# Feed-forward accumulators in four one-bank PSUM tiles, and a new order at the ends of the turns

## Chip, cores and metric

One NeuronCore of one Trainium2 chip runs the whole program. The metric is device time in microseconds (us) of one execution, median of several runs. PE is the matrix engine (TensorE), DVE the vector engine, ACT the scalar engine, POOL GpSimd, and SP the engine whose queue issues most DMAs.

## What is computed

Attention with rotary positions, then a feed-forward block with a squared ReLU, then a gated one, all in fp32 (each fp32 product is made of three passes over a high and a low part):

```python
q_rot, k_rot = rotate(q), rotate(k)                    # q, k, v: (4, 8, 576, 64)
attn = softmax(q_rot @ k_rot.T / 8)
x = (attn @ v).transpose(0, 2, 1, 3).reshape(2304, 512)

r = maximum(x @ w_in, 0)                               # w_in:  (512, 2048), w_out: (2048, 512)
x = (s * r * r + b) @ w_out

g = x @ w_gate                                         # w_gate, w_val: (512, 1536)
return (silu(g) * (x @ w_val)) @ w_out2                # w_out2: (1536, 512)
```

## The kernel before

A planner in the kernel (`Schedule`) holds a list of operations, each with an engine, an assumed duration, a priority, its dependencies, and tokens for the buffers that it takes (`acq`) and gives back (`rel`). `run` walks through modelled time and, on each engine, emits the operation of lowest priority number that is ready and finds its buffers free. What it emits is the order of the instructions on each engine; each engine then works strictly in that order, and the builder adds the semaphore waits that the data and the buffers ask for, tile by tile. So a change of a priority, a dependency or a pool moves instructions all over the later program.

After the attention part the work comes in these stages:

- Block B (`block_b`, which calls `moe1`): the first 512 tokens through the first feed-forward block, in 16 chunks of 128 hidden units. For each chunk, twelve matmuls make `h` (`hb<-x,w`, L844 to L846), ACT and DVE make the activation as a high part `gh` (L901) and a low part `gl` (L906), and twelve matmuls add it into four accumulators (`acc<-gh,w`, the same lines).
- Turn blocks (`block_s(1)`, `block_s(2)`): 768 and 1024 tokens, in two halves. Products of prepared tokens and weights (`hb<-w`) serve both halves in a scheme with seven products in place of eight; `combine` makes the weight pieces (additions L1134, high parts L1140, low parts L1142), `x_load_s` loads the attention result (L1044) and its normalizers (L1059) and prepares the tokens (additions and products L1071, low parts L1083). The first half is accumulated along with the products; its four accumulators are copied out (`y<-acc`, L1194 on DVE and L1196 on ACT); then the second half is accumulated from stored activations, 16 chunks of twelve matmuls (`gh` L1212, `gl` L1215). I call these two parts the first and the second turn.
- Gated blocks (`block_2`, three of them): the same with the second feed-forward block, 768 tokens each, two turns, second projection at L1453 to L1455, copies `o<-acc` at L1468 (DVE) and L1470 (ACT), output DMAs at L1476, token preparation at L1368 to L1379.

PSUM has eight banks. Four are single-bank tiles: three of pool `t` and one of pool `v`, used for `hb`. The other four are two tiles of two banks each, pool `ps_s`: the attention scores use them, and all accumulators after that, two in a tile:

```python
t = ps_s.tile([128, 1024], F32, tag="s", name="acc")
st["acc", h, d], st["acc", h, d + 1] = t[:, 0:QS], t[:, 512:512 + QS]
```

In the gated blocks, which have three accumulators, the second turn starts in the fourth bank, `(c + 3) % 4`. `behind` is what a following block's token preparation waits for in the plan: an activation near the end of the first turn.

Of the kernel before, what the change touches and what calls it, by code (L numbers as in the profile page):

```python
# [8 lines left out]
F32 = mybir.dt.float32  # L9
# [168 lines left out]
def tile_attention_moe_moe(  # L178
# [61 lines left out]
    ps_s = ctx.enter_context(tc.tile_pool(name="ps_s", bufs=2, space=PSUM))  # L240
# [7 lines left out]
    att = ExitStack()  # L248
    at_c = att.enter_context(tc.tile_pool(name="at_c", bufs=1))
# [598 lines left out]
    chains = {"ga": ([], []), "gb": ([], [])}  # L848

    def moe1(st, n, chunks, outs, x_toks, xp, prio, h_pools, get_h, rounds, acc_tok, get_acc, per_bank, gp, rp, pool, engs, rate=1):  # L850

        step = 0
        pend = None
        held = []
        hs, order = chains[gp]
        fin = {}

        def second(pend, rd, first, last):
            f, gops, g_tok, gi = pend
            for z, d in enumerate(rounds[rd]):  # L860
                def fn(z=z, d=d):
                    if first and z == 0:
                        st.setdefault("acc", {}).update(zip(rounds[rd], get_acc(len(rounds[rd]))))
# [3 lines left out]
                    mm3(st["acc"][d], w[:, 0, cs], w[:, 1, cs], gh, gl, first and z % per_bank == 0, last and (z + 1) % per_bank == 0)  # L867
                fin[d] = op("pe", t_mm(n, 3), fn, prio + step * rate, (*gops, W_op["out", f], *order[-1:]), acc_tok[rd] if first and z == 0 else (),
                            (g_tok, W_tok["out", f]))
                order.append(fin[d])  # L870

        for ci, f in enumerate(chunks):
# [11 lines left out]
            r_tok, g_tok = Token(rp), Token(gp)  # L884
            sq_eng = engs
            ew = min(prio + step * rate, EWA) if gp == "ga" else prio + step * rate
            def relu(ci=ci):
                st["g", ci] = tuple(pool(gp).tile([128, 512], F32R, tag=tag, name=tag)[:, 0:n] for tag in ("gh", "gl"))
                st["r", ci] = pool(rp).tile([128, 512], F32, tag="r", name="r")[:, 0:n]
# [33 lines left out]
        for rd in range(1, len(rounds)):  # L923
            for pend in held:
                step += len(rounds[rd])
                second(pend, rd, pend is held[0], pend is held[-1])
# [11 lines left out]
    def switch():  # L938
# [4 lines left out]
        pool("gc", 1)  # L943

# [17 lines left out]
    def block_b():  # L962
# [8 lines left out]
        toks = (Token("s"), Token("s"))  # L971

        def get_acc(m):
            res = []
            for _ in range(2):
                t = ps_s.tile([128, 1024], F32, tag="s", name="acc")
                res += [t[:, 0:UB], t[:, 512:512 + UB]]
            return res

        fin = moe1(st, UB, range(F1), outs, x_toks, xp, prio, ("t", "v"), get_hb,  # L980
                   (tuple(range(KD)),), (toks,), get_acc, 1, "gb", "rb2", lambda name: late[name], "act")
        y_op[0] = []
        for d in range(KD):
            y_tok = Token("rb2", "rc")
            def ev(d=d, y_tok=y_tok):
                st["y", d] = late[y_tok.pool].tile([128, 512], F32, tag="r", name="y")[:, 0:UB]
                nc.scalar.activation(out=st["y", d], in_=st["acc"][d], func=AF.Copy)
            o = op("act", t_act(UB), ev, prio + 900, (fin[d],), (y_tok,), (toks[d // 2],))
# [158 lines left out]
    def block_s(i):  # L1147
# [251 lines left out]
    def block_2(i):  # L1399
# [185 lines left out]

        if not EARLY:
            close()
# [86 lines left out]
```

## Time and profile before

| | us |
|---|---|
| median of 3 runs | 1109.14 |
| lowest and highest run | 1108.8, 1109.45 |
| the profiled execution | 1112.42 |
| its span, first to last instruction | 1110.6 |
| PE busy in the span | 1085.3 (98%), 6218 matmuls |
| DVE busy | 898.2 (81%) |
| ACT busy | 738.6 (67%) |
| mean granted clock of TensorE | 0.995 |

"Busy" is the union of the instructions' times. Matmuls overlap in the pipeline and their ends are modelled, so two matmuls that follow each other without a gap are started one every 0.17 to 0.23 us while each is shown 0.34 to 0.40 us long. What a stretch costs is therefore read from the starts of the matmuls. An idle time in a row is counted from the end of the instruction before on the same engine, with what ended it behind `<-`.

### The profile page before, as it was taken

Reading aid. Unit: us, or ns where it says so; the run is one execution under the profiler, and the core shown is the slowest. Engines: PE = TensorE matmul, PEld = TensorE weight load, DVE = VectorE, ACT = ScalarE, POOL = GpSimd, SP = SyncE. Lnnn points to the kernel's source line nnn. Section 1 sums busy time; section 2 is a strip of 40 time slices with the busy share of each in tenths; the row PEclk is TensorE's granted clock in tenths of the full one; section 3 lists DMA queues with packets and bytes.
Section 4 is the critical chain, followed back from the end, with each engine's and each line's share of the span. In section 5 each row is a group of like instructions: output and inputs, shape, how many; then the busy total and the mean of one; then the engine's idle time right before and its main releaser. Section 6 shows DMA issues by size and latency. Waiting matters only on the chain.

```text
span 1110.6 us, 17632 instructions
## 1 busy us (share of the span) xinstructions
PE 1085.3 (98%) x6218; PEld 986.3 (89%) x6218; DVE 898.2 (81%) x1575; ACT 738.6 (67%) x1511; POOL 202.9 (18%) x166
## 2 busy tenths in 40 slices
PE   8999999999999999989999999999999999999998
PEld 7899999999888799989888878999889998899986
DVE  6999999999988998779899887786586675866750
ACT  5998998999877875546565646665555554655550
POOL 7898877522310000000000000000000000000000
PEclk9999999999999999989999999999999999999999
DMA  4556865654569544572456644231331122311101
GB/s 122 198 187 236 276 213 196 204 183 152 174 206 270 166 163 161 161 199 86 159 189 207 213 160 143 86 114 57 89 92 38 58 81 66 99 41 51 45 17 41
DMA packets 110681, 155.51 MB, mean 140 GB/s; under 512 B 33905, under 2 KB 66689, under 8 KB 110593
## 3 DMA queue, kind: packets, MB, share of 16 engines
q1 hardware_dynamic: 109776, 153.60, 43.3%
q8 instruction: 49, 0.80, 0.3%
q10 hardware_dynamic: 816, 0.79, 0.2%
q14 instruction: 40, 0.32, 0.1%
HBM read 99.98 MB, written 32.58 MB: 119 GB/s over the span
## 4 chain that ended last, share of the span: by engine, by line
PE 85%; DVE 8%; ACT 3%; DMA 2%; issue 1%; SPq 1%; POOL 0%; ACTq 0%; DVEq 0%; POOLq 0%
PE hb L844 13%; PE hb L846 13%; PE hb L845 13%; PE acc L844 6%; PE acc L845 6%; PE acc L846 6%; PE ps_s L652 6%; PE acc L1453 4%; PE acc L1455 4%; PE acc L1454 4%; PE ps_t L713 4%; PE ps_av L743 3%; PE ps_av L745 2%; DVE nm L655 2%; DVE pl L728 2%
## 5 line engine op out<-in xcount | busy, mean ns | idle before, releaser
L844 PE MATMUL hb<-w 128*128 128x384 f32 (+1 forms) x728 | 251.2, 345 | 1.1 <-ACT tmp L1512 0.9
L846 PE MATMUL hb<-w 128*128 128x384 f32 (+1 forms) x728 | 250.4, 344 | 0.0
L845 PE MATMUL hb<-w 128*128 128x384 f32 (+1 forms) x728 | 250.1, 344 | 0.0
L844 PEld LDWEIGHTS hb<-w 128*128 128x128 f32 x728 | 136.7, 188 | 11.5 <-ACT tmp L1512 3.3
L845 PEld LDWEIGHTS hb<-w 128*128 128x128 f32 x728 | 136.7, 188 | 7.4
L846 PEld LDWEIGHTS hb<-w 128*128 128x128 f32 x728 | 136.7, 188 | 4.5
L844 PE MATMUL acc<-gh,w 128*128 128x512 f32 (+1 forms) x320 | 120.8, 377 | 4.9 <-DVE y L1194 3.4
L845 PE MATMUL acc<-gl,w 128*128 128x512 f32 (+1 forms) x320 | 120.1, 375 | 0.7 <-DVE gl L906 0.7
L846 PE MATMUL acc<-gh,w 128*128 128x512 f32 (+1 forms) x320 | 120.1, 375 | 0.0
L655 DVE TENSOR_REDUCE nm<-ps_s 128x1 f32<-128x576 f32 x144 | 108.2, 752 | 8.0 <-PE ps_s L652 6.4
L659 ACT ACTIVATE e<-ps_s,nm 128x576 f32<-128x576 f32 x144 | 106.8, 742 | 8.7 <-DVE nm L655 7.0
L721 ACT ACTIVATE ph<-ps_t 128x512 fp32r<-128x512 f32 x192 | 105.6, 568 | 9.3 <-PE ps_t L713 7.4
L652 PE MATMUL ps_s<-t,a 128*128 128x288 f32 x320 | 99.3, 327 | 4.6 <-ACT e L659 4.4
L743 PE MATMUL ps_av<-ph,vh 128*128 128x384 f32 (+1 forms) x320 | 98.3, 329 | 0.9 <-DVE ph L728 0.5
L728 DVE TENSOR_TENSOR pl<-ps_t,ph 128x512 fp32r<-128x512 f32 x144 | 95.5, 683 | 1.0 <-ACT ph L721 0.2
L1512 ACT ACTIVATE tmp<-hb 128x384 f32<-128x384 f32 x144 | 70.3, 488 | 35.1 <-PE hb L846 33.5
L652 PE MATMUL ps_s<-kz,a 128*128 128x288 f32 x320 | 89.0, 294 | 0.0
L713 PE MATMUL ps_t<-ident,e 128*128 128x128 f32 x576 | 85.7, 273 | 1.9 <-DVE a L565 1.2
L745 PE MATMUL ps_av<-pl,vh 128*128 128x384 f32 (+1 forms) x256 | 75.6, 306 | 0.0
L1142 DVE TENSOR_TENSOR w<-sums,w 128x512 fp32r<-128x512 f32 x104 | 68.5, 686 | 8.1 <-ACT w L1140 8.0
L844 PEld LDWEIGHTS acc<-gh,w 128*128 128x128 f32 x320 | 61.2, 191 | 14.9 <-DVE y L1194 5.1
L713 PEld LDWEIGHTS ps_t<-ident,e 128*128 128x128 f32 x576 | 67.7, 140 | 6.7 <-issue 1.4
(128 smaller groups left out, 2404.9 us busy)
## 6 DMA issues: line engine op xcount, KB each, us to landing
raw<-gv SPq DMA_DIRECT2D x36, 512.0 KB, 3.6
raw<-in_moe_w_out_dram SPq DMA_DIRECT2D x28, 512.0 KB, 3.7
x_d<-xr SPq DMA_DIRECT2D x32, 288.0 KB, 2.7
raw<-in_moe_w_in_dram SPq DMA_DIRECT2D x16, 512.0 KB, 4.4
raw<-up SPq DMA_DIRECT2D x16, 512.0 KB, 4.3
raw<-in_moe_w_gate_dram SPq DMA_DIRECT2D x12, 512.0 KB, 4.2
raw<-in_moe_w_val_dram SPq DMA_DIRECT2D x12, 512.0 KB, 4.2
gv<-dec SPq DMA_DIRECT2D x24, 256.0 KB, 2.2
```

The source lines that it names most:

```text
L652: nc.tensor.matmul(ps[:, hf * 512:hf * 512 + HS], a[:, q0:q0 + 128], m[:, k0:k0 + HS], start=y == 0, stop=y == len(todo) - 1)
L655: nc.vector.tensor_reduce(out=st["nm"][:, u:u + 1], in_=st["s", u], axis=AX.XY, op=ALU.max, negate=True)
L659: nc.scalar.activation(out=st["e", u].rearrange("p (f n) -> p f n", f=2), in_=st["s", u], func=AF.Exp, bias=st["nm"][:, u:u + 1], accum_ou ...
L713: nc.tensor.transpose(ps[:, z * 128:z * 128 + 128], st["e", u][:, kc * 128:kc * 128 + 128], ident)
L721: nc.scalar.activation(out=st["ph", y][0:rows, 512 * i:512 * i + n], in_=st["pt", y, i][0:rows, 0:n], func=AF.Copy)
L728: nc.vector.tensor_tensor(out=dst, in0=st["pt", y, i][0:rows, 0:n], in1=st["ph", y][0:rows, c].bitcast(F32), op=ALU.subtract)
L743: nc.tensor.matmul(ps, vv, st["ph", y][:, c], start=kc == 0, stop=kc == 4)
L745: nc.tensor.matmul(ps, vv, st["pl", y][:, c], start=False, stop=False)
L844: nc.tensor.matmul(o, lh, rh, start=first, stop=False, skip_group_check=more)
L845: nc.tensor.matmul(o, lh, rl, start=False, stop=False, skip_group_check=more)
L846: nc.tensor.matmul(o, ll, rh, start=False, stop=last, skip_group_check=more)
L1512: nc.scalar.activation(out=st[key, f], in_=ps[name], func=AF.Copy)
```

## The change

1. The pool `ps_s` is closed with the attention part, and a pool `acc` of four tiles of one bank each is opened in its place. Each accumulator takes a tile and gives it back by itself.
2. In block B, an activation may use the buffers `gb` or `gc` and `rb2` or `rc`; and in the second to last chunk no second projection is placed, so that those of the last three chunks follow the last `h`.
3. In the turn blocks the first accumulator of the second turn takes a bank of `t` or `v` (an `hb` bank). The first unit's weight combination gets a priority ahead of the token preparation.
4. `behind` also holds the copies of the first turn: the following block's token preparation is placed behind them.
5. In the gated blocks, the activations of the first two chunks of the second turn are formed before the last one of the first turn, in the last block too, and the second turn's first accumulator gets those two before the first turn is closed. The very last copy is done in two halves of 256 columns, one on ACT and one on DVE.

```diff
-    ps_s = ctx.enter_context(tc.tile_pool(name="ps_s", bufs=2, space=PSUM))
+    ps_s = att.enter_context(tc.tile_pool(name="ps_s", bufs=2, space=PSUM))
...
+        pool("acc", 4, space=PSUM)
+
+    def get_acc(n):
+        return late["acc"].tile([128, 512], F32, tag="acc", name="acc")[:, 0:n]
...
-            if pend is not None:
-                second(pend, 0, pend[3] == 0, False)
-                step += len(rounds[0])
-            pend = (f, (o1, o2), g_tok, ci)
-            held.append(pend)
-        second(pend, 0, len(chunks) == 1, True)
+            pend.append((f, (o1, o2), g_tok, ci))
+            while len(pend) > 1 and ci != len(chunks) - 2:
+                x = pend.pop(0)
+                second(x, x[3] == 0, False)
+                step += KD
+        second(pend[0], False, True)
...
-                ("up", u), prio + 60 * (u - 2) + 30, (kept["in", 2 * u], kept["in", 2 * u + 1], W_op["in", F1 - 1], W_op["out", F1 - 1]), (prev,),
+                ("up", u), prio - (701 if i == 1 else 341) if u == 0 else prio + 60 * (u - 2) + 30, (kept["in", 2 * u], kept["in", 2 * u + 1], W_op["in", F1 - 1], W_op["out", F1 - 1]), (prev,),
...
-        acc_tok = {(h, e): Token("s") for h in range(2) for e in range(2)}
+        acc_tok = {(h, d): Token("t", "v") if (h, d) == (1, 0) else Token("acc") for h in range(2) for d in range(KD)}
...
-                    if f == 0 and d % 2 == 0:
-                        t = ps_s.tile([128, 1024], F32, tag="s", name="acc")
-                        st["acc", h, d], st["acc", h, d + 1] = t[:, 0:QS], t[:, 512:512 + QS]
+                    if f == 0:
+                        st["acc", h, d] = get_hb(acc_tok[h, d], QS) if (h, d) == (1, 0) else get_acc(QS)
...
-        behind[i + 1] = pend[1][0]
-        finish(0, fin, prio + 60 * U + 10)
+        behind[i + 1] = (*pend[1][0], *finish(0, fin, prio + 60 * U + 10))
...
-                    o = st["bank"][c if h == 0 else (c + 3) % 4]
+                    o = st["acc", h, c]
...
+                wide = 256 if last and c == nt - 1 else 512
+                both = []
+                for m in range(0, 512, wide):
+                    on_dve = c % 2 or m > 0
...
-        EARLY = 0 if last else 2
-        behind[NB + i + 1] = pend[0]
+        EARLY = 2
...
+            behind[NB + i + 1] = *pend[0], *finish(0, out_proj(0, F2 - 1, prio + 60 * F2 + 10, *pend), prio + 60 * F2 + 10, False)
...
-            o1 = op("act", t_act(QN, False), high, pr, (u2s[f], last_high if f >= max(EARLY, 1) else prev_high), (g_tok,))
+            o1 = op("act", t_act(QN, False), high, pr, (u2s[f], last_high if f >= EARLY else prev_high), (g_tok,))
```

How the order moves, at three places. First DVE at the end of block B, from the next to last low-part of the token preparation on (`gl` is block B's last one, `w<-w` is token preparation, `sums` and the `w` behind them are weight pieces of the turn block). Before:

```order
L1083 TENSOR_TENSOR w<-w 128x768
L906 TENSOR_TENSOR gl<-r,gh 128x512
L1134 TENSOR_TENSOR sums<-raw 128x256
L1083 TENSOR_TENSOR w<-w 128x768
L1142 TENSOR_TENSOR w<-raw,w 128x512
L1134 TENSOR_TENSOR sums<-sums,raw 128x256
L1142 TENSOR_TENSOR w<-raw,w 128x256
L1134 TENSOR_TENSOR sums<-raw 128x256 x2
L1134 TENSOR_TENSOR sums<-raw,sums 128x256
L1142 TENSOR_TENSOR w<-raw,w 128x512
L1134 TENSOR_TENSOR sums<-sums,raw 128x256
L1142 TENSOR_TENSOR w<-sums,w 128x512 x2
```

The same place in the change, where these lines are L1074, L905, L1125 and L1133, and L1062 is an addition of the token preparation:

```order
L905 TENSOR_TENSOR gl<-r,gh 128x512
L1125 TENSOR_TENSOR sums<-raw 128x256
L1133 TENSOR_TENSOR w<-raw,w 128x512
L1125 TENSOR_TENSOR sums<-sums,raw 128x256
L1062 TENSOR_TENSOR w<-w 128x768
L1125 TENSOR_TENSOR sums<-raw 128x256
L1074 TENSOR_TENSOR w<-w 128x768
L1125 TENSOR_TENSOR sums<-raw,sums 128x256
L1074 TENSOR_TENSOR w<-w 128x768
L1133 TENSOR_TENSOR w<-raw,w 128x256
L1133 TENSOR_TENSOR w<-sums,w 128x512 x2
```

One L1071 and one L1083 moved from before the last `gl` to behind it, and one L1142 and two L1134 of the second unit's weights moved behind `w<-sums`.

Second, DVE between the turns of the first turn block: the last `gl`s of the first turn's end, the two copies, and the token preparation of the next block. Before:

```order
L1071 TENSOR_TENSOR w<-w 128x1024
L1215 SCALAR_TENSOR_TENSOR gl<-w,bv,gh 128x384
L1194 COPY y<-acc 128x384
L1071 TENSOR_TENSOR w<-w 128x1024
L1194 COPY y<-acc 128x384
L1215 SCALAR_TENSOR_TENSOR gl<-w,bv,gh 128x384
L1071 TENSOR_TENSOR w<-w 128x1024 x2
```

In the change (L1207 is `gl`, L1184 the copy, L1062 the preparation):

```order
L1207 SCALAR_TENSOR_TENSOR gl<-w,bv,gh 128x384 x2
L1184 COPY y<-acc 128x384 x2
L1062 TENSOR_TENSOR w<-w 128x1024
L1207 SCALAR_TENSOR_TENSOR gl<-w,bv,gh 128x384
L1062 TENSOR_TENSOR w<-w 128x1024
L1207 SCALAR_TENSOR_TENSOR gl<-w,bv,gh 128x384
L1062 TENSOR_TENSOR w<-w 128x1024
L1207 SCALAR_TENSOR_TENSOR gl<-w,bv,gh 128x384
L1062 TENSOR_TENSOR w<-w 128x1024 x2
```

The preparation moved from among the copies to behind them. Before, each copy on DVE waits for ACT; in the change for PE alone.

Third, DVE's last instructions in the change, with the semaphores that they wait for (L1587 forms the last block's stored low parts):

```order
L1587 TENSOR_TENSOR w<-w 128x384 [waits Activation_49] x3
L1455 COPY o<-acc 128x512 [waits DVE_49,PE_49]
L1587 TENSOR_TENSOR w<-w 128x384 [waits Activation_49] x4
L1587 TENSOR_TENSOR w<-w 128x384 [waits DVE_49,Activation_49]
L1455 COPY o<-acc 128x512 [waits DMAHW6_49,DMAHW7_49,DVE_49,PE_49]
L1455 COPY o<-acc 128x256 [waits DMAHW1_49,DMAHW0_49,Activation_49]
```

The last one is DVE's half of the last accumulator, and waits for ACT; before, ACT copied all of it and DVE had no such instruction.

## Rows read from the trace of the kernel before

**Rows 1.** Waits of PE from 330 us on: in total, times, longest.

```profile
PE acc L844 <- DVE y L1194: 3.4, 2, 2.9
PE acc L1453 <- DVE o L1468: 2.4, 3, 0.8
PE acc L844 <- ACT gh L901: 1.3, 1, 1.3
PE hb L844 <- ACT tmp L1512: 0.9, 4, 0.4
...
PE acc L1453 <- ACT o L1470: 0.7, 1, 0.7
```

**Rows 2.** Timeline of PE, end of block B: start, duration, instruction, idle before.

```profile
379.76 0.39 PE L845 MATMUL acc<-gl,w 128*128 128x512 f32 x1
379.99 0.39 PE L846 MATMUL acc<-gh,w 128*128 128x512 f32 x1
381.70 0.50 PE L844 MATMUL acc<-gh,w 128*128 128x512 f32 x1 [1.32 <-ACT gh L901]
...
387.15 0.34 PE L844 MATMUL hb<-w 128*128 128x384 f32 x1
...
389.24 0.33 PE L844 MATMUL hb<-w 128*128 128x384 f32 x1
```

**Rows 3.** Busy time in a window: PE, PEld, DVE, ACT, POOL, granted clock, DMA.

```profile
380.00:390.00 10.00, 7.95 (x31) 6.38 (x30) 10.00 (x21) 8.67 (x17) 0.00 (x0) 0.83 0.26 95
```

**Rows 4.** Timeline of PE between the turns of the first turn block.

```profile
479.02 0.34 PE L846 MATMUL acc<-gh,w 128*128 128x384 f32 x1
...
489.29 0.33 PE L846 MATMUL acc<-gh,w 128*128 128x384 f32 x1
```

**Rows 5.** Timeline of DVE at the same place.

```profile
482.00 1.23 DVE L1071 TENSOR_TENSOR w<-w 128x1024 f32<-128x1024 f32 x1 [2.57 <-DMA w<-x_d]
483.15 0.55 DVE L1194 COPY y<-acc 128x384 f32<-128x384 f32 x1
...
488.32 2.36 DVE L1071 TENSOR_TENSOR w<-w 128x1024 f32<-128x1024 f32 x2 [0.97 <-DMA w<-x_d]
```

**Rows 6.** Timeline of PE between the turns of the first gated block.

```profile
800.22 0.39 PE L1455 MATMUL acc<-w,gl 128*128 128x512 f32 x1
800.68 0.50 PE L1453 MATMUL acc<-w,gh 128*128 128x512 f32 x1
...
801.25 0.40 PE L1455 MATMUL acc<-w,gl 128*128 128x512 f32 x1
802.43 0.50 PE L1453 MATMUL acc<-w,gh 128*128 128x512 f32 x1 [0.78 <-DVE o L1468]
```

**Rows 7.** Timeline of DVE at the same place.

```profile
801.68 0.69 DVE L1468 COPY o<-acc 128x512 f32<-128x512 f32 x1 [0.79 <-PE acc L1455]
```

**Rows 8.** Timeline of DVE, end of block B.

```profile
381.32 0.95 DVE L1083 TENSOR_TENSOR w<-w 128x768 fp32r<-128x768 f32 x1
382.19 0.68 DVE L906 TENSOR_TENSOR gl<-r,gh 128x512 fp32r<-128x512 f32 x1
...
386.28 0.69 DVE L1142 TENSOR_TENSOR w<-raw,w 128x512 fp32r<-128x512 f32 x1
386.88 0.42 DVE L1134 TENSOR_TENSOR sums<-sums,raw 128x256 f32<-128x256 f32 x1
387.21 1.29 DVE L1142 TENSOR_TENSOR w<-sums,w 128x512 fp32r<-128x512 f32 x2
```

**Rows 9.** Groups of DVE, 479 to 519 us: busy us, mean ns, idle before.

```profile
L1071 DVE TENSOR_TENSOR w<-w 128x1024 f32<-128x1024 f32 x10 | 12.0, 1220 | 3.5 <-DMA w<-x_d 3.5
L1215 DVE SCALAR_TENSOR_TENSOR gl<-w,bv,gh 128x384 fp32r<-128x384 f32 x14 | 8.6, 615 | 1.1 <-ACT gh L1212 1.0
L1083 DVE TENSOR_TENSOR w<-w 128x1024 fp32r<-128x1024 f32 x7 | 8.4, 1220 | 0.0
```

**Rows 10.** Groups of ACT, 470 to 520 us, and ACT's last copy in the timeline.

```profile
L1196 ACT ACTIVATE y<-acc 128x384 f32<-128x384 f32 x4 | 2.0, 488 | 3.7 <-DMA raw<-up 2.8 <-PE acc L846 0.9
...
1106.49 0.60 ACT L1470 ACTIVATE o<-acc 128x512 f32<-128x512 f32 x1 [17.07 <-PE acc L1455]
```

More of the change, by code (lines that the diff above doesn't have):

```diff
@@ L846, in mm3, with moe1, second, fn @@
         nc.tensor.matmul(o, ll, rh, start=False, stop=last, skip_group_check=more)
-    chains = {"ga": ([], []), "gb": ([], [])}
-    def moe1(st, n, chunks, outs, x_toks, xp, prio, h_pools, get_h, rounds, acc_tok, get_acc, per_bank, gp, rp, pool, engs, rate=1):
+    chains = {"gb": ([], [])}
+    def moe1(st, n, chunks, outs, x_toks, xp, prio, h_pools, get_h, acc_tok, gp, rp, pool, engs, rate=1):
         step = 0
-        pend = None
-        held = []
-        hs, order = chains[gp]
+        pend = []
+        hs, order = chains["gb"]
         fin = {}
-        def second(pend, rd, first, last):
+        def second(pend, first, last):
             f, gops, g_tok, gi = pend
[L860 to L863, printed above, removed]
+            for d in range(KD):
+                def fn(d=d):
+                    if first:
+                        st["acc", d] = get_acc(n)
                     w = W["out", f]
@@ L866, in fn @@
                     gh, gl = st["g", gi]
-                    mm3(st["acc"][d], w[:, 0, cs], w[:, 1, cs], gh, gl, first and z % per_bank == 0, last and (z + 1) % per_bank == 0)
-                fin[d] = op("pe", t_mm(n, 3), fn, prio + step * rate, (*gops, W_op["out", f], *order[-1:]), acc_tok[rd] if first and z == 0 else (),
+                    mm3(st["acc", d], w[:, 0, cs], w[:, 1, cs], gh, gl, first, last)
+                fin[d] = op("pe", t_mm(n, 3), fn, prio + step * rate, (*gops, W_op["out", f], *order[-1:]), (acc_tok[d],) if first else (),
                             (g_tok, W_tok["out", f]))
@@ L883, in moe1, with relu @@
                 step += 1
-            r_tok, g_tok = Token(rp), Token(gp)
+            r_tok, g_tok = Token(*rp), Token(*gp)
             sq_eng = engs
[L886 to L889, printed above, removed]
+            ew = prio + step * rate
+            def relu(ci=ci, r_tok=r_tok, g_tok=g_tok):
+                st["g", ci] = tuple(pool(g_tok.pool).tile([128, 512], F32R, tag=tag, name=tag)[:, 0:n] for tag in ("gh", "gl"))
+                st["r", ci] = pool(r_tok.pool).tile([128, 512], F32, tag="r", name="r")[:, 0:n]
                 nc.scalar.activation(out=st["r", ci], in_=st["h", ci], func=AF.Relu)
@@ L1180, in fn @@
                     mm3(st["acc", h, d], w[:, 0, cs], w[:, 1, cs], gh, gl, f == 0, f == F1 - 1)
-                res.append(op("pe", t_mm(QS, 3), fn, pr + d, (*gops, W_op["out", f], *order[-1:]), (acc_tok[h, d // 2],) if f == 0 and d % 2 == 0 else (),
+                res.append(op("pe", t_mm(QS, 3), fn, pr + d, (*gops, W_op["out", f], *order[-1:]), (acc_tok[h, d],) if f == 0 else (),
                               (g_tok, W_tok["out", f])))
@@ L1429, in bank @@
             return p.tile([128, 512], F32, tag=tag, name="hb")[:, 0:QN]
-        a_toks = (Token("s"), Token("s"))
-        evs = {}
-        def get():
-            st["bank"] = []
-            for _ in range(2):
-                t = ps_s.tile([128, 1024], F32, tag="s", name="acc2")
-                st["bank"] += [t[:, 0:512], t[:, 512:1024]]
+        a_toks = {(h, c): Token("acc") for h in range(2) for c in range(nt)}
         def out_proj(h, f, pr, gops, g_tok, chunks=None):
-            def need(c):
-                return (evs[0, c - 1],) if h == 1 and f == 0 and c > 0 else ()
             res = []
@@ L1446, in fn @@
                 def fn(c=c):
-                    if f == 0 and c == 0 and h == 0:
-                        get()
+                    if f == 0:
+                        st["acc", h, c] = get_acc(512)
                     w = o_st[f]
@@ L1476, in put @@
                         e.dma_start(out=out[b * S:(b + 1) * S].rearrange("(r g) m -> r g m", g=PC)[:, g], in_=st["y", h, c][64 * z:64 * z + 64])
-                    sch.dma(131072, put, pr, (o,), (), (y_tok,), eng="act" if other else "sp")
+                    sch.dma(131072, put, pr, both, (), (y_tok,), eng="act" if other else "sp")
+            return evs
         t_tok = {}
```

63 lines of the change are left out of this document (27 added, 36 removed).

## The prediction

> **What bounds the kernel now.** I read the page first: TensorE (PE) has work in flight for 1085.3 of 1110.6 us, so a gain can only come out of stretches in which PE starts nothing. PE's list of waits after the attention part gives those that this change touches, all around the accumulators of the feed-forward blocks [rows 1]: the copies `y` on DVE, the copies `o` on DVE and on ACT, and an activation `gh` of the first block. These rows count idle time from the modelled end of a matmul; what a wait costs is read from the starts. Undisturbed, PE starts a 512-column matmul every 0.23 us and a 384-column one every 0.174 us (387.15 to 389.24 are twelve steps) [rows 2].
>
> Place A, the end of block B. From 379.99 to 387.15 PE starts 13 matmuls in 7.16 us [rows 2]; 13 x 0.227 = 2.95, so 4.21 us are lost, part of it as a lower clock: the granted clock is 0.83 in that 10 us stretch, some of it at the lower of its two levels after the idle time, while DVE has work for 10.00 of 10.00 us [rows 3]. PE waits there for the last chunk's activations.
>
> Place B, between the two turns of the first turn block (`block_s(1)`). From 479.02 to 489.29 PE starts 24 matmuls in 10.27 us [rows 4]; 24 x 0.174 = 4.18, so 6.09 us are lost. DVE's timeline tells why: an addition of the token preparation (L1071) sat 2.57 us for a load from `x_d`, and the copy L1194 that PE needs stood behind it and came at 483.15 [rows 5]; PE's longest wait for it is 2.9 us [rows 1].
>
> The other places: the second wait for `y` is 3.4 - 2.9 = 0.5 [rows 1]. At 800.68 the step is 0.46 in place of 0.23 (0.23 lost), and at 802.43 it is 1.18 (0.95 lost, of which 0.78 is shown as idle, so a shown wait costs about 0.17 more than it says) [rows 6]. The `o` L1468 wait occurs three times (2.4 in all) and the `o` L1470 one once (0.7) [rows 1]. DVE's copy at 801.68 had itself been held 0.79 us by PE [rows 7]: it reads one bank of a two-bank tile, and waited for matmuls into the other bank.
>
> **The change part by part, by place.**
>
> *A, activations a step ahead.* Twelve more matmuls (the second projection of the chunk before) stand between the last first-projection matmul and the last second projection; no matmul is added. So the last activations have 24 x 0.227 = 5.45 us where they had 2.7. But DVE is full. Before the last `gl`, the order takes two preparation instructions away, 0.87 us each (381.32 to 382.19), so `gl` ends at about 382.87 - 1.74 = 381.1 where PE would reach it at 380.45: 0.7 us of waiting stay. The next thing that is late is the weight piece `sums` (L1142) for the third product of the turn block; in before it starts at 387.21. The change takes one L1142 and two L1134 from in front of it, 0.60 + 0.33 + 0.33 = 1.27 us [rows 8]; the first unit's combination is also planned ahead of the token preparation, but DVE still must do all of both. So it ends at 387.21 - 1.27 + 0.69 = 386.6, and the third product starts at about 386.7, not 389.24 [rows 2]. Gain 2.55 of 4.21, 1.65 stay. Bounds: nothing gained if DVE had to do the same work in front of it, all 4.21 if it found room. I take the middle because the two lists of DVE are known instruction by instruction and DVE has no idle time there.
>
> *B, preparation behind the copies.* Two additions (L1071, 1.22 us each [rows 9]) that stood among the last `gl`s of the first turn move behind the two copies; the two copies follow each other. Nobody in front of a copy waits for a load any more. The first accumulator of the second turn gets a bank of its own kind (an `hb` bank), the other three follow copies that are 3, 6 and 9 matmuls old, so the entry costs nothing. What waits next: the addition that needs the last `x_d` piece now holds `gl`s of the second turn. In before the addition could start at 488.32, after 0.97 us of waiting for the load, which is 9.1 us after the turn's first matmul (nominally 479.02 + 0.17 = 479.2) [rows 4, 5]. The SP queue of the change issues the loads of the first token rows later and the following ones earlier, with the same bytes; I take 6.7 to 9.1 us. Behind it stand one multiplication and `gl` of chunk 5: 2 x 1.15 + 0.6 later, 9.6 to 12.0, and PE wants it after five chunks of 12 x 0.174, at 10.4. Then two multiplications and the next `gl`, 2.9 against PE's 2.1: 0.8 more. So 0 to 2.4 us of waiting, I take 1.2. Gain 6.09 - 1.2 = 4.9; if the loads come 1 us later than in before, 3.5 stay.
>
> *One bank for each accumulator, and the turn order of the gated blocks.* The second `y` wait goes with its 0.17: 0.67. In each of the two inner gated turns (800 and the same at 942) both steps go, 2 x 1.18 = 2.36: the first copy no longer waits for the neighbouring bank's matmuls, and the second starts when its own bank is done, about a step and a half before PE wants it. In the last block the wait of 0.7 (0.87) goes because two chunks of the second turn are now done before the close, and the third L1468 wait (0.95) because a free bank is taken. Together 4.85. What covers the copies, if they were later: nine matmuls, 2 us.
>
> *Fewer waits for buffers in block B* (`gc` and `rc` added to the choices): no wait of PE names them; 0, from -0.5 to 0.5.
>
> *The last copy in two halves.* The last ACT copy takes 0.60 us, and the last DMA is issued straight behind it [rows 10]. The halves are 256 columns. From the 384-column copies, 0.49 on ACT [rows 10] and 0.55 on DVE [rows 5], and the 512-column ones, 0.60 and 0.69 [rows 7, 10], 256 columns are 0.38 and 0.42 (estimates along the slope). The built order makes DVE's half wait for ACT's: 0.80 + 0.04 = 0.84, so 0.24 us are lost. Side by side they would end after 0.42 and win 0.18. The Trainium skill (PSUM — Partial Sum Buffer, section on bank collisions) says that two engines must not touch one bank in the same partitions at the same time, two reads included, while different banks are free: by that, halves of one bank have to take turns, and only halves of two banks would win. The wait in the order agrees; without it the sum below would be 0.4 us lower.
>
> Everything else is moved, not added: PE has the same number of matmuls, DVE one instruction more. The waits of products for `tmp` (0.9 in all [rows 1]) I leave as they are.
>
> Sum: 2.55 + 4.9 + 4.85 - 0.24 = 12.1 us. The profiled execution's span is 1110.6 and it took 1112.42 us; the median of the runs is 1109.14, 3.3 below it. Taken off the span, 1098.5; off the median, **1097.0 us**.
>
> **The rivals.** *All of it comes back*: DVE finds room at A and the loads land early at B. 4.21 + 6.09 + 4.85 + 0.2 = 15.35 off: 1093.8. For it: neither wait is one for arithmetic that PE depends on by nature. Against it: DVE's 10.00 of 10.00.
>
> *DVE becomes the bound at the entries of the turn blocks*: the third product at A comes no earlier than now (4.21 stay), B keeps 3.5, and the reshuffled DVE order costs another 1 us somewhere later. 15.15 - 8.7 - 0.24 = 6.2 off: 1102.9. For it: in the second turn at B, DVE has 12 L1071 and 7 L1083 of 1.22, 16 `gl` of 0.615 [rows 9] and about 4.2 of weights, 37 us, in a turn of 192 x 0.174 = 33.4. Against it: the last 5 us of this are needed only after the third product of the next block, 2.7 us past the turn's end.
>
> *Slower, by that same queue*: with the preparation wholly inside the second turn, a late load delays every `gl` behind it, then the next block's products, and the clock falls again. By the count above it has some 1 us of slack beyond a landing at 9.1 us; each further us is a us of PE. It turns the whole change slower by over 2.2 us when that piece lands 14 us later, about 23 us into the turn: then about 1112. For it: the loads in front of it are all in one queue, and their order is changed. Against it: nothing adds bytes.
>
> *Nothing happens*: the builder still ties the copies to neighbours or the planner's new order makes as many small waits as it takes away: 1109. Against it: the DVE copies of the change wait for PE alone.
>
> **How the numbers follow.** Forecast 0.60; all back 0.12; DVE the bound 0.17; nothing 0.05; slower 0.06. A measurement of this kernel tells about 0.2%, 2.2 us, from no change (its runs lie within 0.7 us). Faster: 0.60 + 0.12 + 0.17 = 0.89; the same 0.05; slower 0.06. The range takes in the full return (1093.8, less 0.3) and the DVE case (1102.9, plus 0.6): 1093.5 to 1103.5, and leaves out the last two cases and the tails.
>
> **What would show it.** PE's waits without `y` and `o`; at B the copies on DVE side by side with nothing between them, and a wait of PE for `gl` (L1207 in the change) of 0 to 2.4 us some 10 us into the turn; at A a `gl` wait of 0.7 and a wait of a product for a weight piece of about 1; a granted clock of 1.0 around both; DVE's 256-column copy starting as ACT's ends. Wrong would be: PE waits of over 4 us for `gl` or for products at the next block's entry, or the copies still starting after other engines' work.

## The result and the profile after

The change takes the median from 1109.3 us (4 runs, 1108.8 to 1113.51) to **1098.03 us** (4 runs, 1096.49 to 1099.74). The ratio is 0.9891 with a 95% interval of 0.9862 to 0.9919: faster by 0.8 to 1.4%. The forecast was 1097.0, in a range of 1093.5 to 1103.5. The total came out near the forecast; its parts did not, as the runs below show.

The head of the profile page and the busy times of the changed kernel:

```profile
span 1096.5 us, 17621 instructions
## 1 busy us (share of the span) xinstructions
PE 1078.2 (98%) x6218; PEld 984.6 (90%) x6218; DVE 897.3 (82%) x1576; ACT 736.7 (67%) x1511; POOL 204.8 (19%) x166
```

PE's waits from 330 us on, against [rows 1]:

```profile
PE hb L844 <- ACT tmp L1237: 0.5, 1, 0.5
PE hb L844 <- ACT w L1237: 0.4, 1, 0.4
```

All waits for `y`, `o`, `gh`, `gl` and for the gated blocks' `tmp` are gone in this profile, the last also, which the forecast had left standing. Two short ones are new: products at the entry of the first turn block, in PE's timeline (against [rows 2]):

```profile
388.34 0.34 PE L846 MATMUL hb<-w 128*128 128x384 f32 x1
389.16 0.45 PE L844 MATMUL hb<-w 128*128 128x384 f32 x1 [0.48 <-ACT tmp L1237]
...
393.98 0.45 PE L844 MATMUL hb<-w 128*128 128x384 f32 x1 [0.38 <-ACT w L1237]
```

From start to start these cost 0.65 and 0.55 us (389.16 - 388.34 - 0.174, and the same at 393.98). The granted clock of the window that had 0.83 [rows 3] is 1.00:

```profile
380.00:390.00 10.00, 9.52 (x46) 7.92 (x45) 9.97 (x18) 9.08 (x18) 0.00 (x0) 1.00 0.32 113
```

DVE between the turns of the first turn block, against [rows 5]: the two copies stand side by side, each waits for PE alone, and the preparation comes behind.

```profile
479.09 0.55 DVE L1184 COPY y<-acc 128x384 f32<-128x384 f32 x1
479.92 0.56 DVE L1184 COPY y<-acc 128x384 f32<-128x384 f32 x1 [0.29 <-PE acc L846]
480.40 1.22 DVE L1062 TENSOR_TENSOR w<-w 128x1024 f32<-128x1024 f32 x1
```

The end, against [rows 10]: two halves one behind the other, 0.83 us from 1092.14 to the end of the second (the forecast's estimate: 0.84; before: 0.60).

```profile
1092.14 0.38 ACT L1457 ACTIVATE o<-acc 128x256 f32<-128x256 f32 x1 [16.09 <-PE acc L1436]
1092.55 0.42 DVE L1455 COPY o<-acc 128x256 f32<-128x256 f32 x1 [8.09 <-ACT o L1457]
```

One thing does not fit: the spans differ by 1110.6 - 1096.5 = 14.1 us, the medians by 11.3. The profiled execution of the kernel before lay 3.3 us above its median, and the first 300 matmuls, in which the programs are the same, took 38.83 us there and 41.94 here. So the experiments begin with both kernels once more.

### The profile page after: what moved, and what is told of

It is laid out like the page before. It is cut to its first block, busy times and chain, and to the rows that moved or that the text cites. A ratio compares the mean times of both kernels' runs of the same rounds, so it can differ in the third digit from the quotient of the medians.

```text
span 1096.5 us, 17621 instructions
## 1 busy us (share of the span) xinstructions
PE 1078.2 (98%) x6218; PEld 984.6 (90%) x6218; DVE 897.3 (82%) x1576; ACT 736.7 (67%) x1511; POOL 204.8 (19%) x166
## 4 chain that ended last, share of the span: by engine, by line
PE 64%; DVE 0%; ACT 0%; issue 0%
PE hb L844 13%; PE hb L846 13%; PE hb L845 12%; PE acc L1436 5%; PE acc L1435 5%; PE acc L1434 5%; PE acc L846 4%; PE acc L845 4%; PE acc L844 4%; DVE o L1455 0%; ACT o L1457 0%
## 5 line engine op out<-in xcount | busy, mean ns | idle before, releaser
L846 PE MATMUL acc<-gh,w 128*128 128x512 f32 (+1 forms) x288 | 106.8, 371 | 0.0
L845 PE MATMUL acc<-gl,w 128*128 128x512 f32 (+1 forms) x288 | 106.8, 371 | 0.0
L844 PE MATMUL acc<-gh,w 128*128 128x512 f32 (+1 forms) x288 | 106.7, 371 | 0.0
L1133 DVE TENSOR_TENSOR w<-sums,w 128x512 fp32r<-128x512 f32 x104 | 68.2, 684 | 8.5 <-ACT w L1131 8.3
L652 PEld LDWEIGHTS ps_s<-t,a 128*128 128x128 f32 x320 | 60.4, 189 | 8.4 <-ACT e L659 7.1
```

The costliest lines, as they stand in the source:

```text
L652: nc.tensor.matmul(ps[:, hf * 512:hf * 512 + HS], a[:, q0:q0 + 128], m[:, k0:k0 + HS], start=y == 0, stop=y == len(todo) - 1)
L844: nc.tensor.matmul(o, lh, rh, start=first, stop=False, skip_group_check=more)
L845: nc.tensor.matmul(o, lh, rl, start=False, stop=False, skip_group_check=more)
L846: nc.tensor.matmul(o, ll, rh, start=False, stop=last, skip_group_check=more)
```

## The experiments

**Both kernels again.** No edit.

> The kernel before, unchanged, timed and profiled a second time, because the two profiled executions differ by 14.1 us in span and the medians by 11.3. Theory 1 (the opening varies from execution to execution): the feed-forward part has the same gaps again (about 4.2 us at the end of block B, 5 to 6 at the first turn change, 1.18 at each gated turn change), and only the start of the attention part in front of 20 us moves, by up to 3 us. Theory 2 (the gap at the first turn change hangs on the landing of a load and was unusually long in the first profile): it is shorter by 2 us or more here, and the opening is the same.

> The changed kernel, unchanged, a second time. Theory 1: 1096.5 to 1100 us, no gap above 0.7 us behind the attention part, the same two waits of 0.5 and 0.4 us behind block B; the opening may be up to 3 us shorter than in the first profile, and the ratio comes out at 0.988 to 0.991. Theory 2: the opening is the slow one again, because the change made it so; then the opening of the kernel before stays the fast one, and the ratio is that of the first measurement.

Measured: 1108.55 us for the kernel before (12 runs, 1107.03 to 1110.98; ratio to the other runs of it 0.9989, 0.9974 to 1.0004), 1097.8 us for the changed one (6 runs; 0.9899, 0.9877 to 0.9921). Both theories held in part: the start moved (theory 1, 38.83 to 40.25 us) and so did the gap at the first turn change (theory 2). PE's waits in the second profile of the kernel before:

```profile
PE acc L844 <- DVE y L1194: 0.7, 2, 0.5
...
PE hb L844 <- ACT tmp L1245: 0.6, 1, 0.6
PE hb L844 <- ACT w L1245: 0.2, 1, 0.2
```

The second profile of the changed kernel has the two short waits at the entry again (0.6 and 0.4), and a third at the end of block B:

```profile
PE acc L845 <- DVE gl L905: 0.3, 1, 0.3
```

In the kernel before, the wait for `y` is 0.7 us where it was 3.4 [rows 1]. DVE's timeline there has the same order as [rows 5], but the addition between the two copies found its load landed:

```profile
480.30 0.56 DVE L1194 COPY y<-acc 128x384 f32<-128x384 f32 x1 [0.22 <-ACT y L1196]
480.78 1.22 DVE L1071 TENSOR_TENSOR w<-w 128x1024 f32<-128x1024 f32 x1
481.91 0.55 DVE L1194 COPY y<-acc 128x384 f32<-128x384 f32 x1
```

The DMA traffic in the same 5 us differs too. The first profile of the kernel before, and then the second, in which PE gets to the same matmul 1.4 us later (the last three columns are granted clock, DMA share and GB/s):

```profile
480.00:485.00 5.00, 2.07 (x9) 1.74 (x8) 3.00 (x4) 0.39 (x1) 0.00 (x0) 0.73 1.06 285
```

```profile
480.00:485.00 5.00, 4.61 (x25) 3.96 (x24) 4.78 (x7) 2.40 (x5) 0.00 (x0) 1.00 1.06 336
```

The DMA engines were full in both (1.06), and moved 285 GB/s in one and 336 in the other. The slowest of the `x_d` loads issued between 455 and 500 us took 12.6 us from issue to landing in the first profile and 7.7 in the second. Why the rate differed is open.

The kernel before lost as much time in both profiles at place A, though not in the same way. The window that had a granted clock of 0.83 in the first profile [rows 3] has 1.00 in the second, behind the same waits for `gh` (1.3) and `gl` (0.7):

```profile
380.00:390.00 10.00, 7.40 (x33) 5.61 (x31) 9.96 (x19) 9.23 (x18) 0.00 (x0) 1.00 0.15 54
```

PE came to the turn block's products sooner there, and waited for banks that ACT had to copy out (the `tmp` and `w` waits above). The stage took 80.35 us in place of 80.53: the lower clock of the first profile cost the stage next to nothing.

The table gives the time between the starts of the same numbered matmuls of PE in all four profiles:

| stage (matmul numbers) | before, 1st | before, 2nd | after, 1st | after, 2nd |
|---|---|---|---|---|
| start of attention (0 to 300) | 38.83 | 40.25 | 41.94 | 39.44 |
| attention, most of block B (300 to 2350) | 281.10 | 281.25 | 280.99 | 280.76 |
| A, end of block B, entry of the turn block (2350 to 2700) | 80.53 | 80.35 | 78.20 | 79.10 |
| B, first turn change (3100 to 3300) | 40.85 | 35.69 | 34.75 | 34.75 |
| second turn change (3800 to 4000) | 47.21 | 47.21 | 46.19 | 46.19 |
| entry of the first gated block (4000 to 4200) | 40.06 | 40.04 | 39.25 | 39.23 |
| two gated turn changes, with the entries behind them (4600 to 5600) | 198.90 | 198.88 | 194.66 | 194.66 |
| last turn change to the end (6000 on) | 47.69 | 47.70 | 45.56 | 45.56 |
| the other four stretches | 329.97 | 329.62 | 329.22 | 329.17 |
| start of the last matmul to the end of the span | 4.57 | 4.57 | 4.81 | 4.83 |

Two rows vary between executions of one program: the start, and place B of the kernel before, by 5.2 us. The rest repeats to 0.2 us for the kernel before (0.35 in the last but one row, which is four stretches), and to 0.25 for the changed one, with 0.9 at A. Of 23 more runs of the kernel before, 19 took 1106.7 to 1110.4 us and four 1113.2 to 1114.4; whether a load was late in those four no trace shows.

**The order at the first turn change.** Once the preparation is put back ahead of the second copy in the changed kernel, once the hold on the copies is added to the kernel before. Both edits do the same in the second turn block and in the gated blocks. The first of them, without its hunk for the gated blocks:

```diff
-        behind[i + 1] = (*pend[1][0], *finish(0, fin, prio + 60 * U + 10))
+        behind[i + 1] = pend[1][0]
+        finish(0, fin, prio + 60 * U + 10)
...
```

> The changed kernel with the token preparation held by the activation alone, as before: at the first turn change a preparation step stands between the last activations and the copies again, though every accumulator has a bank of its own. Theory 1 (the copy is late because the in-order DVE queue holds a preparation step that waits for a load): PE loses 2.5 to 4 us again at the first turn change, and the time is 2.5 to 4 us above the changed kernel, some 1101.5 us. Theory 2 (the tie between the two banks of a tile made the copy late, and the order on DVE matters little): no gap above 1 us there and the time of the changed kernel within 1 us.

> The kernel before with one thing of the change: the next block's token preparation is held by the copies of the first turn. Two-bank accumulators stay. Theory 1: of the 6.1 us at the first turn change 5 to 6 go, the 1.18 us at each gated turn change and the 4.2 us at the end of block B stay; 5 to 6 us under the kernel before, about 1103.5 us. Theory 2 (the tie is the cause): at least 3 us stay at the first turn change, and the time is within 3 us of the kernel before.

Measured: 1098.25 us without the hold (0.9907, 0.9884 to 0.9929) and 1107.5 us for the hold alone (0.9986, 0.9973 to 0.9999). Beside the second runs of the kernels that they start from (1097.8 and 1108.55), taking the hold out costs 0.5 us and putting it in gains 1.1, with intervals that overlap. The times are as theory 2 has them, yet the second gap that it left standing in the kernel before is not there either (at the first turn change with the hold alone, one step of PE is 0.29 us too long, and the matmul behind it starts 0.11 late). Theory 1 missed both times, because no load was late in the two profiled executions; so they could not tell what a late load does.

Away from the first turn change the traces do show something that the hold is worth. Without it, PE waits at the entry of the first gated block of the changed kernel:

```profile
PE hb L844 <- ACT tmp L1502: 0.8, 1, 0.8
```

The matmuls 4000 to 4200 take 40.39 us there, against 39.25 and 39.23 in the two profiles of the changed kernel.

**A load made late.** In three kernels the `x_d` load of one quarter of the tokens is issued twice.

```diff
-                    for h in range(2):
+                    for h in (0, 1, 0, 1) if i == 2 and home == "t3" else (0, 1):
```

> The kernel before, with the x_d load of one quarter of the next block's tokens issued twice (the same bytes to the same place), so that the preparation step that stands between the two DVE copies of the first turn change gets its operand some 3 to 6 us later. Theory A (the 6.1 us in the first profile were a load that landed late, ahead of a copy that PE needs): PE loses 3 to 6 us at the first turn change again, where the second profile of the kernel before lost 0.72; 1111.5 to 1115 us. Theory B (the lateness of the copy had another cause): under 1.5 us there, and the time within 1 us of the kernel before.

> The changed kernel with the same load issued twice. Theory A: the copies stand ahead of the preparation and nothing is lost at the turn change itself; a late step then holds a gl of the second turn, 0 to 3 us of PE some 8 to 12 us into the turn: 1098 to 1101 us. Theory B: no difference to the changed kernel.

> The changed kernel with the preparation ahead of the second copy again (not held by the copies), and the load issued twice. Theory A1 (the order on DVE is what protects PE from a late load): 3 to 5 us lost at the first turn change, 1101 to 1103 us. Theory A2 (the separate banks protect it: the second turn begins in an hb bank, its other three accumulators take the banks of the first three copies, and nobody soon needs the bank of the fourth copy, the one behind the late step): the copy is late and PE does not wait for it; what is lost is at most what the changed kernel loses with the late load, within 1 us of that.

Measured: 1117.57 us for the kernel before (1.0074, 1.005 to 1.0098), 1101.27 for the changed one (0.9925, 0.9901 to 0.9948), 1102.9 without the hold (0.994, 0.992 to 0.996). DVE in the kernel before with the late load:

```profile
484.99 1.23 DVE L1071 TENSOR_TENSOR w<-w 128x1024 f32<-128x1024 f32 x1 [4.58 <-DMA w<-x_d]
486.13 0.55 DVE L1194 COPY y<-acc 128x384 f32<-128x384 f32 x1
```

That is the picture of [rows 5] made at will, and PE waits 5.0 us for the copy. Theory A holds as to the cause; the kernel before lost more than it said (7.2 us of stage time against the second profile, where 3 to 6 were expected, and a time 2.6 us above its range), because the matmuls behind the wait ran at a lower granted clock (last section). For the changed kernel the time lies 0.3 us above the range of theory A. The changed kernel with the late load: DVE first, then PE's timeline.

```profile
486.88 2.36 DVE L1062 TENSOR_TENSOR w<-w 128x1024 f32<-128x1024 f32 x2 [3.63 <-DMA w<-x_d]
489.16 0.61 DVE L1207 SCALAR_TENSOR_TENSOR gl<-w,bv,gh 128x384 fp32r<-128x384 f32 x1
```

```profile
489.82 0.44 PE L845 MATMUL hb<-gl,w 128*128 128x384 f32 x1 [1.56 <-DVE gl L1207]
492.62 0.44 PE L845 MATMUL hb<-gl,w 128*128 128x384 f32 x1 [0.42 <-DVE gl L1207]
```

The wait has moved from the copies to two `gl`s in the second turn, and is shorter: start to start 1.72 and 0.59. Without the hold, DVE's second copy stands behind a wait of 4.23 us, nearly that of the kernel before (4.58), but PE does not wait for it; it waits 1.93 us for the `gl` behind it:

```profile
483.61 1.23 DVE L1062 TENSOR_TENSOR w<-w 128x1024 f32<-128x1024 f32 x1 [4.23 <-DMA w<-x_d]
484.76 0.55 DVE L1184 COPY y<-acc 128x384 f32<-128x384 f32 x1
485.22 0.61 DVE L1207 SCALAR_TENSOR_TENSOR gl<-w,bv,gh 128x384 fp32r<-128x384 f32 x1
```

```profile
485.89 0.44 PE L845 MATMUL hb<-gl,w 128*128 128x384 f32 x1 [1.93 <-DVE gl L1207]
```

Theory A2 holds as to the copy, but not as to the time, which is 1.6 us above the changed kernel and inside the range of theory A1. The time between matmuls 3100 and 3300 is 42.92 us in the kernel before, 38.52 without the hold and 37.32 with it (34.75 with no late load), so in these executions the hold was worth 1.2 us there; at the entry of the first gated block it was worth 1.15 again (40.40 without it, 39.25 with it). The intervals of the two times overlap.

**The hb bank.** The kernel without the hold, with the late load, and with the second turn's first accumulator in one of the four accumulator banks.

```diff
-        acc_tok = {(h, d): Token("t", "v") if (h, d) == (1, 0) else Token("acc") for h in range(2) for d in range(KD)}
+        acc_tok = {(h, d): Token("acc") for h in range(2) for d in range(KD)}
...
```

> The kernel of the run before with the late load and the preparation ahead of the second copy, with one more thing undone: the first accumulator of the second turn takes one of the four accumulator banks again and not an hb bank, so that the fourth accumulator of the second turn needs the bank of the fourth copy, the one behind the late step. DVE has the same order of instructions at the turn change. Theory A2 (the hb bank is what kept PE going there): PE waits for that copy at its tenth matmul of the second turn, 4 to 5 us, in place of the 2.1 us that it lost to a gl later; some 3 us more, 1105 to 1106.5 us. Theory A4 (one bank for each accumulator is enough): no wait for a copy, 2.1 us for the gl, the same time within 1 us.

Measured: 1104.96 us (10 runs; 0.9958, 0.9945 to 0.9971), about 2 us more than with the hb bank, with intervals that overlap. The trace decides: the matmuls 3100 to 3300 take 41.35 us, 2.8 more than with the hb bank. PE's wait there:

```profile
PE acc L844 <- DVE y L1184: 4.0, 1, 4.0
```

DVE's order at the turn change is that of the kernel without the hold and with the late load. So it is the fifth bank that takes the fourth copy off PE's path: theory A2 again.

**Banks only.** The chunk order, the priority of the first weight combination, the hold, the steps ahead in the last block and the split copy are undone. The kernel keeps, beside the four tiles and the hb bank, the wider choice of buffers in block B, and that of the gated blocks' two early activations, which may take any free slot.

```diff
-            while len(pend) > 1 and ci != len(chunks) - 2:
+            while len(pend) > 1:
...
-        EARLY = 2
+        EARLY = 0 if last else 2
...
-                wide = 256 if last and c == nt - 1 else 512
+                wide = 512
```

> The changed kernel with everything undone but the accumulators of one bank each (with the hb bank for the first accumulator of the second turn): old order of the last chunks of block B, old priority of the first weight combination, preparation not held by the copies, the last gated block's activations not a step ahead, the last copy whole. Theory C (the banks are what gains at all turn changes, at the entries of the gated blocks too): no gap above 0.5 us at any turn change nor at the gated blocks' entries, at the end of block B the 3.6 us of the kernel before instead of 1.9, and the last copy 0.24 us shorter: about 1099.3 us. Theory D (the order of the work is needed too): gaps of 0.9 us and more come back at the turn change of the last gated block (0.85) and at the first turn change; 1101 us or more.

Measured: 1099.29 us (0.9903, 0.9881 to 0.9925). PE's waits:

```profile
PE hb L846 <- DVE w L1133: 1.2, 2, 0.6
PE hb L844 <- ACT w L1237: 0.3, 1, 0.3
PE hb L844 <- ACT tmp L1502: 0.2, 1, 0.2
```

No wait at any turn change: theory C, and the time that it gave (1099.3). So these banks, with what the kernel keeps beside them, make some 10 of the 11 us. At the end of block B theory C was wrong. The old chunk order did not bring the `gh` and `gl` waits back: the planner now puts the turn block's first products ahead of the last second projection, and PE waits for their weight pieces instead. From matmul 2350 to 2700 it takes 79.26 us, beside 78.20 and 79.10 in the changed kernel and 80.35 before.

**The chunk order alone, and the last block alone.** The first two edits of the diff above, one at a time.

> The changed kernel with the old order of the last chunks in block B alone (the second projection of a chunk placed behind each h, two and not three chunks of it behind the last h). Theory E (the longer run of matmuls covers the last activations): a wait for gh of 1.3 us and one for gl of 0.7 to 1 come back at the end of block B, some 1.7 us more than the changed kernel, about 1099.5 us. Theory F (DVE sets the entry of the turn block, wherever PE waits): PE waits for gh and gl instead of for the products' banks behind, the sum is the same within 0.5 us, and so is the time.

> The changed kernel with the last gated block closed as before (the second turn's first two activations and projections not ahead of the closing of the first turn). If the two steps ahead are what removed the wait of 0.85 us at that turn change, it comes back: 0.8 to 0.9 us more. If the free fourth bank removed it, no gap above 0.3 us there and the time of the changed kernel.

Measured: 1098.57 us with the old chunk order (5 runs; 0.9903, 0.9886 to 0.992), 1097.47 us with the old last block (4 runs; 0.989, 0.9877 to 0.9904): neither can be told from the changed kernel. With the old chunk order PE's waits at the entry are for banks that ACT must copy out:

```profile
PE hb L844 <- ACT tmp L1237: 1.7, 2, 1.3
```

From 2350 to 2700 it takes 79.18 us, so the sum is that of theory F; but PE does not wait for `gh` and `gl`, as both theories had it, because twelve matmuls of the turn block's products stand ahead of the last second projection here too. In the last block there is no gap above 0.15 us at the turn change: the free fourth bank removed that wait, not the steps ahead.

**A version with two more edits.**

```diff
-                wide = 256 if last and c == nt - 1 else 512
+                wide = 512
...
             o = op("act", t_act(UB), ev, prio + 900, (fin[d],), (y_tok,), (toks[d],))
+            if d > 1:
+                held_y.append(o)
...
-                return op("act", t_act(QS), fn, pr, (o,), (tok,) if tok is not None else ())
+                o = op("act", t_act(QS), fn, pr, (o,), (tok,) if tok is not None else ())
+                if i == 1 and u == 0:
+                    while held_y:
+                        o.users.append(held_y[-1])
+                        held_y.pop().need += 1
+                return o
```

> The changed kernel with two edits: the last copy whole on ACT again, and two of the four copies of block B's result placed behind the first copy of the turn block's products on ACT. The first shortens the end, from the last matmul to the last copy's end, by 0.24 us (0.84 to 0.60 plus the same waits). The second: if ACT's queue sets the two waits of 0.5 to 0.8 us at the entry of the turn block, the first of them shrinks by 0.3 to 0.8 us; if the DVE queue sets them (weight pieces), it stays. In all 0.2 to 1.0 us under the changed kernel.

Measured: 1096.17 us (4 runs, 1096.0 to 1096.96; 0.9882, 0.9868 to 0.9895). It is the lowest median of all, 1.6 us under the changed kernel where 0.2 to 1.0 were expected; the intervals overlap, and the trace accounts for 0.25 us alone. The last copy and the first of the two output DMAs behind it:

```profile
1090.32 0.60 ACT L1465 ACTIVATE o<-acc 128x512 f32<-128x512 f32 x1 [16.09 <-PE acc L1444]
1090.94 0.47 SPq L1472 DMA_DIRECT2D out_dram<-o  x1
```

0.62 us from the copy's start to the issue, where the two halves take 0.87 in the second profile of the changed kernel (1090.22 to 1091.09): the split copy costs 0.25 us. The other edit gave nothing that the trace shows: the first wait at the entry became one for a weight piece (0.31 from start to start), the second grew to 1.07, 1.38 in all. The stage takes 78.61 us, between the two of the changed kernel: ACT's copies and DVE's weight pieces are both just late there.

## Why the prediction was right, and which steps were not

The total of 12.1 us stands against 11.3 by the first medians and 10.8 by the second (1108.55 - 1097.8). By the second pair of profiles the parts are 10.6 us behind the attention (table: A 1.25, B 0.94, second turn change 1.02, first gated entry 0.81, the two gated blocks 4.22, the last block 2.14, the rest 0.45, the end -0.26). So 12.1 was reached with errors of both signs: 4.0 us too much at B and 1.3 at A, and 3.3 too little in the turn changes and entries behind B, which gained 8.2 where 4.85 were forecast. That these nearly cancel is luck. Of the signs that the prediction named, the `y` and `o` waits are gone, DVE's copies stand side by side, the granted clock is 1.00 and DVE's last half starts as ACT's ends; the waits at A are other ones.

- **B failed.** The step was "Gain 6.09 - 1.2 = 4.9". The 6.09 were real in that one execution, and their cause was read rightly: a late load, a DVE queue in order, a copy behind it. But the step took a load's lateness in one profile as the kernel's usual state. In the second profile it is not there, and the gain at B is 0.94 us. The hint stood in the prediction itself: the profiled execution lay 3.3 us above the median. The 1.2 us of `gl` waits forecast for the change did not come either (0 in both profiles); they come with a late load, as two waits of 1.72 and 0.59.
- **The tmp waits were missed.** The step was to leave "the waits of products for `tmp`" as they are, at 0.9 us. At the inner entries they belonged to the same tie between banks. In the kernel before, ACT's timeline at a gated block's entry (the copy, then the `tmp` copy that PE waits for):

```profile
826.33 0.60 ACT L1470 ACTIVATE o<-acc 128x512 f32<-128x512 f32 x1 [0.47 <-DVE o L1468]
826.83 0.62 ACT L1140 ACTIVATE w<-raw 128x512 fp32r<-128x512 f32 x1
827.35 0.48 ACT L1512 ACTIVATE tmp<-hb 128x384 f32<-128x384 f32 x1
```

In the changed kernel at the same place:

```profile
816.25 0.60 ACT L1457 ACTIVATE o<-acc 128x512 f32<-128x512 f32 x1 [0.50 <-PE acc L1436]
817.29 0.49 ACT L1501 ACTIVATE tmp<-hb 128x384 f32<-128x384 f32 x1 [0.44 <-PE hb L846]
```

ACT's copy had waited for DVE's copy of the neighbouring bank and held `tmp` behind it. From start to start these waits cost 0.37 and 0.26 at each inner entry and 0.54 at the first one in the second profile of the kernel before: 1.80 us, twice what the idle times say. The waits at the inner entries are gone with the banks alone too. The one at the first entry hangs on the hold as well: it was 0.36 from start to start with the banks alone, and without the hold alone there is one of 0.92 six matmuls later.
- **The banks' 4.85 were right in kind and too small.** Both steps at the inner gated turn changes (0.23 and 0.95, together 1.18), 0.86 and 0.95 in the last block and the steps at the second turn change are gone. But each such wait costs about 0.11 more than the forecast counted, because the matmul behind it is late as well: in [rows 6] two steps take 0.57 us from 800.68 to 801.25, where 0.46 are undisturbed. By the stages these turn changes gained about 6 us without the `tmp` waits. One reason was wrong: the wait of 0.87 goes because a fourth bank is free, not because two chunks are done before the close.
- **A failed in its mechanism and was too large.** It was forecast at 2.55, from activations a step ahead, and is 2.33 in the first pair of profiles and 1.25 in the second. DVE is full there in all four (9.96 to 10.00 of 10.00 us between 380 and 390 us), as the step argued; but the waits that stay are for banks behind ACT's copies, with the weight piece just behind them (it takes over in the last experiment); a `gl` wait of 0.3 in place of 0.7 is in one profile of two; and the new chunk order is not what gains: with the old one the stage takes 79.18 us, beside 78.20 and 79.10. Nor was the clock part of what could be won there: at a granted clock of 1.00 the kernel before takes 80.35 us, at 0.83 it took 80.53. Which of the banks and the wider choice of buffers does it was not tried apart, nor was the priority of the first weight combination tried alone.
- **The end was right**: -0.24 forecast, -0.24 and -0.26 measured. ("The sum below would be 0.4 us lower" has its sign the wrong way round: without the wait the gains would add up to more, and the time would be lower.) The halves took turns in the built order; the Trainium skill (PSUM — Partial Sum Buffer, section on bank collisions) asks for that in one bank. No run here shows two engines in one bank at once.
- **The rivals.** "All of it comes back" is out: A keeps 1.2 us of waits from start to start, and the lowest run of the changed kernel is 1096.4. "Nothing happens" is out: in the trace the copies wait for their own bank alone. "DVE becomes the bound" was in part true at A, where putting the old chunk order back hardly moves the stage. The rival on the slower side named the right queue but had the balance reversed: a late load costs the changed kernel some 3.5 us (1101.27 - 1097.8), but the kernel before some 7.9 (1117.57 - 1109.72).

## What to carry to other kernels

Before a long wait for a DMA is priced as a gain, compare the profiled execution's time with the median, and take a second profile: a wait that is in one and not in the other is an event, and the change is worth what is left without it. Where engines copy out of tiles that matmuls still write, give each accumulator a tile of its own: the tie runs from bank to bank and from engine to engine, and its cost is found also where the waits bear other names. Where a turn begins while the last one is still copied out, a spare bank takes the last copy off the path, whatever stands before it in its queue: with a late load it was worth 2.8 us at the first turn change here, and the order 1.2 beside it.

## What was not expected of the hardware

With the DMA engines full, the rate between 480 and 485 us of the same program was 285 GB/s in one execution and 336 in another, and the slowest `x_d` load there took 12.6 us to land and 7.7. That the rate is what made the load late is not shown. The first 300 matmuls, the same in all these programs, took 38.8 to 41.9 us in the four profiles above.

The granted clock behind a wait differed from case to case. The kernel before with the late load, in the window in which its wait of 5.0 us ended, and the changed kernel with the late load, in the window of its wait of 1.56 us and in the next:

```profile
485.00:490.00 5.00, 3.26 (x10) 3.26 (x11) 4.76 (x6) 0.93 (x2) 0.00 (x0) 0.55 1.05 325
```

```profile
485.00:490.00 5.00, 3.44 (x20) 3.12 (x19) 3.12 (x4) 0.73 (x1) 0.00 (x0) 1.00 1.07 337
490.00:495.00 5.00, 4.58 (x25) 4.26 (x26) 5.00 (x6) 4.05 (x7) 0.00 (x0) 1.00 0.28 108
```

After 5.0 us of idle time PE ran near the lower of its two levels (0.55), after 1.56 at the higher one (1.00). So the long wait cost more than its length: the stage took 42.92 us, 7.2 more than in the second profile of the kernel before (35.69). The wait of 1.93 us in the kernel without the hold had 0.67 in the window from 485.00 on. Nor does the length of a wait settle it: behind the same waits of 1.3 and 0.7 us at the end of block B, the kernel before had 0.83 between 380 and 390 us in its first profile and 1.00 in its second.
